# Pinning TensorE's order in the main batches of a fused attention, GLU and soft-MoE kernel

## The chip, the core and the metric

The kernel runs on one core of a Trainium2 chip. A core has five engines with a queue of instructions each: TensorE (PE in the profile; its weight loads are PEld), VectorE (DVE), ScalarE (ACT), GpSimd (POOL) and SyncE (SP), which here mostly issues transfers. TensorE writes its products to PSUM, eight banks of 128 x 512 float32, from which the other engines read them. The metric is the time of one execution in microseconds (us), lower is better; the profile describes one further execution.

## The reference

Three layers follow each other. An attention reads 8 batches of 512 tokens (8 heads of 64) against 32 states per head in both directions, which gives 512 + 32 rows of 512 numbers per batch, 4352 rows in all. A gated layer normalizes each row, multiplies it by two matrices of 512 x 1536 and combines them. A soft mixture of experts gathers 32 slots out of all rows, runs 8 experts on them and spreads the result back over the rows.

```python
a  = softmax(scale * x @ state.T);  xread = a @ state
a2 = softmax(scale * state @ x.T);  sread = a2 @ x
x  = concat([xread, sread])                          # 4352 rows of 512
xn = x / sqrt(mean(x*x) + 1e-6) * rms_g
y  = (silu(xn @ w_gate) * (xn @ w_val)) @ w_out      # 512 -> 1536 -> 512
logits = y @ phi                                     # 32 slots
d  = softmax(logits, over rows);  slot = d.T @ y     # 32 x 512
out = softmax(logits, over slots) @ experts(slot)    # 4 slots per expert
```

## The kernel before

The 4096 rows of xread are worked on in eight batches g = 0 to 7 of 512 rows; the 256 rows of sread follow as a group of their own, then the experts and the output. In a batch the gated layer runs in 12 *units* (c, t): c = 0 to 2 is a third of the 1536 columns, t = 0 to 3 a tile of 128 rows. A unit has six matmuls of 128 x 512 for the gate (`main_mm(g, c, t, 0)`, L85, tile `mm<-wp,A`), a silu on ScalarE (`main_silu`, L566, `sg`), six matmuls for the value (`main_mm(g, c, t, 1)`), and the product of both on VectorE (`main_h`, L574, `h`). The matrices `wp` are the weights multiplied by the batch's state, in a high and a low part, so they are made anew for each batch: `sw(b, c, gv)` runs two groups of small tiled products (`misc<-w,stTg`, L85), and each half is copied by ScalarE (cast, L537) and then subtracted by VectorE (L538). There are six `sw` per batch.

TensorE's other work per batch, all of it through the `misc` banks: `h_T` (L111), four transpositions of an h tile, copied to `hT` by ScalarE or VectorE (L585); `lg_mm`, the logits of a third of the columns (into a bank of its own, `lg`); `post2` and `post3`, the softmax over rows kept up to date, with small VectorE and ScalarE operations (L630 to L656) and the transpositions of E and L (L669, L670); `slot_h`, three products of h with E; and the steps of the attention for the next two batches: `att_gram`, `att_b1` (transpositions of sT), `att_b2` (`misc<-xn,e2T`), `att_b3` (transposition of srd, which VectorE computes in L360), `att_q` (`misc<-A,G`), `att_v`, `att_ss`, and `att_a3` (`misc<-xT,stT`: two banks, each read by a maximum on VectorE, L255 `cm`, and then a copy on ScalarE, L257). `c_exp` and `post_exp` run exponentials on ScalarE, for which it loads another table (ACT_TABLE_LOAD) and back again for the silu.

The program is written as `stages`: stage 0 has the 16 units of batch 0 and of the first third of batch 1, stage 1 the other 8 units of batch 1, and stages 2 to 7 one batch each. Which extra step is written beside which unit stands in `plan`, filled by `at(u, slot, step)`: slot 1 lies between a unit's gate and value products, slot 2 behind it. `next_turned()` picks up to two units whose h is turned (`h_T`) inside a later unit. The written order is only where a scheduler starts from: apart from the start of the program it orders each engine's instructions itself, by its own idea of what is ready. PSUM has four banks for the main products (`mmps`), three for all else (`misc`) and one for the logits.

Of the kernel before, what the change touches and what calls it, by code (L numbers as in the profile page):

```python
# [8 lines left out]
F32 = mybir.dt.float32  # L9
# [11 lines left out]
def kernel(  # L21
# [17 lines left out]
    B, P, H, NT, D = x_n.shape  # L39
# [38 lines left out]
    def mmps():  # L78
        return psp.tile([P, 512], F32, tag="mm", bufs=4, name="mm")

    def misc():
        return psp.tile([P, 512], F32, tag="misc", bufs=3, name="misc")
# [812 lines left out]

    for s, units in enumerate(stages):
# [67 lines left out]
        else:  # L964
            g = s
            o = 4 if s == 1 else 0
            if s == 1:
                at(0, 1, conv1)
                at(0, 2, wphi_part, 2, 1)
            nxt = [(g, 1), (g, 2)] + ([(g + 1, 0)] if g + 1 < B else [])  # L970
            for i, (nb, c) in enumerate(nxt):
                if 4 * i >= o:
                    at(4 * i - o, 2, sw, nb, c, 0)
                    at(4 * i - o + (2 if i == 1 and g > 1 else 1), 1 if i == 1 and g > 1 else 2, sw, nb, c, 1)
            if g < 7:
                at(4 if g == 1 else 1, 1, wload, 1)
                at(6 if g == 1 else 2, 2, wconv, 1)
            if g + 1 < B:
                nb = g + 1
                at(1, 1, load_xn, nb)  # L980
                at(1, 2, att_exp, nb, g > 1)
                if g > 1:
                    at(1, 2, c_exp, g - 2, True)
                    at(2, 1, c_norm, g - 2)
                at(1, 2, att_norm, nb)
                at(0, 1, att_gram, nb)
                if g > 1:
                    at(2, 2, att_b1, nb)
                    at(4, 1, att_b4, nb)
                    at(5, 2, att_b2, nb)  # L990
                    at(6, 2, att_b3, nb)
                    at(6, 2, att_q, nb, 0)
                    at(7, 1, att_q, nb, 1)
                    at(8, 2, att_v, nb)
                    at(9, 2, att_ss, nb)
                    at(10, 1, rinv, nb)
                else:
                    at(4, 2, att_b1, nb)
                    at(6, 1, att_b2, nb)
                    at(6, 2, att_b3, nb)  # L1000
                    at(5 - o // 2, 2, att_b4, nb)
                    at(6 - o // 2, 1, att_q, nb, 0)
                    at(6 - o // 2, 2, att_q, nb, 1)
                    at(7 - o // 2, 1, att_v, nb)
                    at(7 - o // 2, 2, att_ss, nb)
                    at(8 - o // 2, 1, rinv, nb)
                at(6 - o, 1, att_g, nb)
            elif g > 1:
                at(0, 1, c_exp, g - 2)
                at(0, 1, c_norm, g - 2)  # L1010
            if g + 2 < B:
                nb = g + 2
                at((8 if g > 1 else 6) - o, 1 if g > 1 else 2, load_xt, nb)
                at((10 if g > 1 else 8) - o, 1 if g > 1 else 2, att_a3, nb)
                at(11 - o, 2, att_a4, nb)
                at(10 - o, 1, att_z, nb)
            if g == B - 1:
                at(0, 2, prefetch, 2)
                at(8, 1, prefetch, 2)
                at(11, 1, w_split, 0, 0)  # L1020
                at(12, 2, w_split, 1, 0)
            if g == B - 2:
                at(8, 2, sread_prep)

        for u, (g, c, t) in enumerate(units):
# [14 lines left out]
            if ends(now):  # L1040
# [5 lines left out]
                for i in range(NC):  # L1046
                    at(u + 4, 1, slot_h, pg, i)
# [371 lines left out]
```

## Time and profile before

| | |
|---|---|
| time, median of 3 runs | 667.89 us (667.5, 667.89, 668.51) |
| the profiled execution: own time, span | 667.35 us, 665.5 us |
| mean granted TensorE clock | 0.969 |
| TensorE busy | 615.7 us, 93% of the span |
| VectorE, ScalarE, GpSimd busy | 424.4 us (64%), 338.3 us (51%), 158.3 us (24%) |
| main matmuls of the batches | 1152, 306.7 us |
| batches 2 to 7, from the first main matmul of batch 2 | 182.5 to 537.3 us |
| sread's main matmuls, then experts and output | 537.3 to 570, 570 to 665.5 us |

Busy time is the sum of an engine's instructions, without what it waits. TensorE's share is an average over stages; in the batches it is higher than at the end, where the experts' weights and the output are moved. In a timeline a row is a run of like instructions with its start and its length; the end of a run of matmuls is modelled, so the start of the next row is the surer mark. A bracket such as [0.81 <-PE misc L85] is the engine's idle time ahead of the row and what ended it.

### The profile page before, as it was taken

Reading aid. Unit: us, or ns where it says so; the run is one execution under the profiler, and the core shown is the slowest. Engines: PE = TensorE matmul, PEld = TensorE weight load, DVE = VectorE, ACT = ScalarE, POOL = GpSimd, SP = SyncE. Lnnn points to the kernel's source line nnn. Section 1 sums busy time; section 2 is a strip of 40 time slices with the busy share of each in tenths; the row PEclk is TensorE's granted clock in tenths of the full one; section 3 lists DMA queues with packets and bytes.
Section 4 is the critical chain, followed back from the end, with each engine's and each line's share of the span. In section 5 each row is a group of like instructions: output and inputs, shape, how many; then the busy total and the mean of one; then the engine's idle time right before and its main releaser. Section 6 shows DMA issues by size and latency. Waiting matters only on the chain.

```text
span 665.5 us, 11200 instructions
## 1 busy us (share of the span) xinstructions
PE 615.7 (93%) x4436; PEld 385.8 (58%) x4436; DVE 424.4 (64%) x874; ACT 338.3 (51%) x551; POOL 158.3 (24%) x178
## 2 busy tenths in 40 slices
PE   6796989999999999999999999999999999999980
PEld 4444566555656756566666666575666777653360
DVE  6969899675698566656856685686764265242170
ACT  5466784575356446434734553384445476311180
POOL 2635364532034012302210140222000000003420
PEclk9698998999999999999999999999999999999995
DMA  9950065132031212203020320300093028999757
GB/s 355 414 206 1 1 246 197 64 127 68 1 119 72 68 43 86 100 1 126 2 100 0 128 95 2 128 0 33 10 371 122 5 96 273 316 337 393 292 208 328
DMA packets 32715, 92.14 MB, mean 138 GB/s; under 512 B 1816, under 2 KB 3224, under 8 KB 29848
## 3 DMA queue, kind: packets, MB, share of 16 engines
q1 hardware_dynamic: 32376, 91.36, 37.2%
q8 instruction: 35, 0.57, 0.3%
q14 instruction: 16, 0.13, 0.1%
q10 hardware_dynamic: 288, 0.07, 0.0%
HBM read 79.37 MB, written 12.06 MB: 137 GB/s over the span
## 4 chain that ended last, share of the span: by engine, by line
PE 50%; DVE 20%; issue 18%; ACT 6%; POOL 3%; DMA 1%; DVEq 0%; POOLq 0%; ACTq 0%
PE mm L85 27%; PE misc L85 12%; PE misc L111 6%; PE so L85 2%; PE lg L85 2%; DVE h L574 2%; DVE w L212 2%; DVE wp L538 1%; POOL A L468 1%; DVE asum L326 1%; DVE wo L212 1%; DVE cm L255 1%; DVE w L208 1%; DVE w L204 1%; DVE a L268 1%
## 5 line engine op out<-in xcount | busy, mean ns | idle before, releaser
L85 PE MATMUL mm<-wp,A 128*128 128x512 f32 x1152 | 306.7, 407 | 2.3 <-ACT sg L566 1.2
L85 PEld LDWEIGHTS mm<-wp,A 128*128 128x128 f32 x1152 | 207.7, 190 | 88.1 <-issue 43.7
L566 ACT ACTIVATE sg<-mm,rinv 128x512 f32<-128x512 f32 x102 | 70.6, 692 | 105.3 <-PE mm L85 90.9
L574 DVE SCALAR_TENSOR_TENSOR h<-mm,rinv,sg 128x512 f32<-128x512 f32 x102 | 75.5, 743 | 61.6 <-PE mm L85 55.3
L538 DVE TENSOR_TENSOR wp<-misc,wp 128x512 fp32r<-128x512 f32 x96 | 62.2, 684 | 55.5 <-ACT wp L537 55.5
L537 ACT CAST wp<-misc 128x512 fp32r<-128x512 f32 x96 | 51.7, 591 | 75.6 <-PE misc L85 75.6
L85 PE MATMUL misc<-w,stTg 64*32 64x512 f32 x768 | 66.3, 611 | 10.2 <-POOL w L216 5.9
L585 ACT COPY hT<-misc 128x512 f32<-128x512 f32 x86 | 49.4, 584 | 45.2 <-PE misc L111 41.0
L111 PE MATMUL misc<-ident,h 128*128 128x128 f32 x408 | 61.0, 275 | 6.7 <-DVE h L574 6.1
L111 PEld LDWEIGHTS misc<-ident,h 128*128 128x128 f32 x408 | 48.0, 141 | 26.7 <-ACT sg L566 5.1
L511 POOL TENSOR_TENSOR rinv<-ri,rs_magic 128x4 int32<-128x4 int32 (+1 forms) x9 | 1.8, 197 | 154.9 <-DVE ri L507 154.9
L216 POOL TENSOR_TENSOR w<-w,raw 128x512 int32<-128x512 int32 x20 | 28.2, 1422 | 29.9 <-issue 8.8
L85 PEld LDWEIGHTS misc<-w,stTg 64*32 64x32 f32 x768 | 10.9, 105 | 41.6 <-issue 17.6
L85 PE MATMUL mm<-wh,xsg 128*128 128x512 f32 x96 | 31.7, 400 | 0.0
L216 POOL TENSOR_TENSOR wo<-wo,raw 128x512 int32<-128x512 int32 x18 | 24.8, 1393 | 26.7 <-DVE wo L212 20.3
L329 POOL TENSOR_TENSOR a<-a,asum 128x1024 f32<-128x1024 f32 x7 | 13.4, 1916 | 69.5 <-DVE cs L710 59.0
L85 PE MATMUL lg<-hT,wphi 128*32 128x512 f32 (+1 forms) x216 | 28.2, 578 | 0.0
L1165 POOL MEMSET sinE<- 128x512 f32 x2 | 1.0, 524 | 111.4 <-PE mm L85 101.3
L85 PE MATMUL misc<-h,ET 128*32 128x512 f32 x204 | 26.6, 597 | 0.0
L191 ACT ACTIVATE raw<-raw 128x1024 int32<-128x1024 uint32 x19 | 22.0, 1160 | 0.0
L85 PEld LDWEIGHTS mm<-wh,xsg 128*128 128x128 f32 x96 | 17.9, 188 | 6.7 <-issue 3.1
L693 DVE SCALAR_TENSOR_TENSOR acc<-acc,al,misc 128x512 f32<-128x512 f32 (+1 forms) x24 | 17.8, 746 | 4.5 <-PE misc L85 2.9
(219 smaller groups left out, 836.5 us busy)
## 6 DMA issues: line engine op xcount, KB each, us to landing
ew<-in_w_dram SPq DMA_DIRECT2D x27, 1024.0 KB, 7.3
xT<-in_x_t_dram SPq DMA_DIRECT2D x8, 1024.0 KB, 4.9
xn<-in_x_n_dram SPq DMA_DIRECT2D x8, 1024.0 KB, 4.9
raw<-in_w_val_dram SPq DMA_DIRECT2D x6, 1024.0 KB, 16.0
raw<-in_w_out_dram SPq DMA_DIRECT2D x6, 1024.0 KB, 4.9
out_dram<-ob SPq DMA_DIRECT2D x6, 1024.0 KB, 11.7
ew_w<-in_w_dram SPq DMA_DIRECT2D x5, 1024.0 KB, 10.6
raw<-in_w_gate_dram SPq DMA_DIRECT2D x4, 1024.0 KB, 13.8
```

The costliest lines, as they stand in the source:

```text
L85: nc.tensor.matmul(out=o, lhsT=lhsT, rhs=rhs, start=start, stop=stop)
L111: nc.tensor.transpose(o, i, ident)
L191: ins = nc.scalar.activation(out=rnd, in_=lo.bitcast(U32), func=AF.Copy, scale=2.0 ** -29)
L212: nc.vector.scalar_tensor_tensor(out=a[:, h], in0=hi[:, h], scalar=-0x40000000, in1=a[:, h], op0=ALU.bitwise_and, op1=ALU.bitwise_or,)
L216: nc.gpsimd.tensor_tensor(out=a[:, h], in0=a[:, h], in1=rnd[:, h], op=ALU.add)
L329: (eng or nc.gpsimd).tensor_tensor(out=a3, in0=a3, in1=asum.unsqueeze(2).to_broadcast([P, 32, 32]), op=ALU.mult)
L537: nc.scalar.copy(t[:, r, 0, :], ps)
L538: nc.vector.tensor_tensor(out=t[:, r, 1, :], in0=ps, in1=t[:, r, 0, :].bitcast(F32), op=ALU.subtract)
L566: nc.scalar.activation(out=sg, in_=ps, func=AF.Silu, scale=RINV[g][:, t : t + 1])
L574: nc.vector.scalar_tensor_tensor(out=HH[g, c][:, t, :], in0=ps, scalar=RINV[g][:, t : t + 1], in1=sg, op0=ALU.mult, op1=ALU.mult,)
L585: (nc.vector.tensor_copy if on_dve else nc.scalar.copy)(HT[g, c][:, :, t * P : (t + 1) * P], ps.rearrange("p (q n) -> p q n", q=4))
L693: nc.vector.scalar_tensor_tensor(out=acc[:np_, c, :], in0=acc[:np_, c, :], scalar=Q[g, "al"][:np_], in1=ps[:np_, :], op0=ALU.mult, op1=ALU ...
```

## The change

The change takes effect from stage 2 on, with one exception: the banks of PSUM are shared out anew for the whole program, three for main products and four for the rest. From the first unit of batch 2 to the last of batch 7 TensorE's instructions stay in the order in which they are written; the other engines are still ordered by the scheduler. Two units' main products, 24 matmuls, are written in a row; behind every second unit comes a *burst*, one of six lists per batch that `steady(g)` returns, with all of TensorE's other work. h_T and lg_mm are no longer written inside the units. The steps that don't use TensorE (loads, exponentials, norms) stay in `plan`. From batch 3 to 6, `att_b2` and `att_b3` of a batch stand in the first burst of that same batch; those of batch 7 stand in batch 6. The `else` branch of the plan, which served stages 1 to 7, keeps only what it had for stage 1 (left out below).

```diff
-        return psp.tile([P, 512], F32, tag="mm", bufs=4, name="mm")
+        return psp.tile([P, 512], F32, tag="mm", bufs=3, name="mm")
 
     def misc():
-        return psp.tile([P, 512], F32, tag="misc", bufs=3, name="misc")
+        return psp.tile([P, 512], F32, tag="misc", bufs=4, name="misc")
...
+    pe_order = ExitStack()
+
+    def steady(g):
+
+        nb, nn = g + 1, g + 2
+        last = g == B - 1
+
+        def turn(c, t, dve=False):
+            return (h_T, g, c, t, dve)
+
+        bursts = [[] for _ in range(6)]
+        b = bursts[0]
+        b += [(post2, g - 1)]
+        if not last:
+            b += [(att_gram, nb)]
+        b += [(post_exp, g - 1), (c_exp, g - 2, True)]
+        if 2 < g < B - 1:
+            b += [(att_b2, g), turn(0, 0, True), (att_b3, g)]
+        else:
+            b += [turn(0, 0, True)]
+        b += [(sw, g, 1, 0)]
+        b = bursts[1]
+        b += [(sw, g, 1, 1), (post3, g - 1), turn(0, 1), turn(0, 2)]
+        if not last:
+            b += [(att_b1, nb)]
+        b = bursts[2]
+        b += [turn(0, 3), turn(1, 0)] + [(slot_h, g - 1, i) for i in range(NC)]
+        if g == B - 2:
+            b += [(att_b2, nb)]
+        b += [(lg_mm, g, 0, 3), (sw, g, 2, 0)]
+        b = bursts[3]
+        b += [(sw, g, 2, 1)]
+        if not last:
+            b += [turn(1, 1), (att_q, nb, 0), turn(1, 2), (att_q, nb, 1)]
+        else:
+            b += [turn(1, 1), turn(1, 2)]
+        if g == B - 2:
+            b += [(att_b3, nb)]
+        b = bursts[4]
+        b += [turn(1, 3)]
+        if nn < B:
+            b += [(att_a3, nn)]
+        b += [turn(2, 0)]
+        if not last:
+            b += [(att_v, nb), (att_ss, nb), (rinv, nb), (sw, nb, 0, 0)]
+        else:
+            b += [(lg_mm, g, 1, 3)]
+        b = bursts[5]
+        if not last:
+            b += [(sw, nb, 0, 1), turn(2, 1), turn(2, 2), turn(2, 3, True)]
+            b += [(lg_mm, g, 1, 3), (lg_mm, g, 2, 3), (post1, g)]
+            if g == B - 2:
+                b += [(sread_prep,)]
+            ended.add(g)
+        else:
+            b += [turn(2, 1), turn(2, 2)]
+
+        at = lambda u, slot, f, *a: plan.setdefault((base + u, slot), []).append((f, a))
+        at(2, 1, c_norm, g - 2)
+        if not last:
+            at(1 if g == B - 2 else 7, 1, load_xn, nb)
+            at(1, 1, att_exp, nb, True)
+            at(2, 1, att_norm, nb)
+            at(4, 1, att_b4, nb)
+            at(6, 1, att_g, nb)
+            at(1, 1, wload, 1)
+            at(4, 1, wconv, 1)
+        if nn < B:
+            at(8, 1, load_xt, nn)
+            at(9, 1, att_z, nn)
+            at(11, 1, att_a4, nn)
+        if last:
+            at(0, 2, prefetch, 2)
+            at(8, 1, prefetch, 2)
+            at(11, 1, w_split, 0, 0)
+            at(12, 2, w_split, 1, 0)
+
+        return bursts
...
+                pe_order.enter_context(tc.manual_schedule(engines={mybir.EngineType.PE}))
+            bursts = steady(s)
...
-            now = next_turned()
+            now = next_turned() if s < 2 else pend[:] if (s, u) == (2, 0) else []
...
-                at(u + 1, 1, post2, pg)
-                at(u + 1, 1, post_exp, pg)
-                at(u + 2, 2, post3, pg)
-                for i in range(NC):
-                    at(u + 4, 1, slot_h, pg, i)
+                if s < 2 and u + 1 < len(units):
+                    at(u + 1, 1, post2, pg)
+                    at(u + 1, 1, post_exp, pg)
+                    at(u + 2, 2, post3, pg)
+                    for i in range(NC):
+                        at(u + 4, 1, slot_h, pg, i)
             run(2)
             pend = pend[len(now) :] + [(g, c, t)]
+            if s > 1:
+                if u % 2:
+                    for f, *a in bursts[u // 2]:
+                        f(*a)
+                pend = [(g, c, t)] if g == B - 1 and u == 11 else []
...
+        if s == B - 1:
+            pe_order.close()
```

On TensorE, in batch 4 around the third `sw` (the one that reads `w_559`), the order before has runs of six mains with a step between them:

```order
L85 MATMUL misc<-w_559,stTg 32x512 x8
L85 MATMUL mm<-wp_2809,A_2588 128x512 x6
L111 MATMUL misc<-ident,h_2991 128x128 x4
L85 MATMUL mm<-wp_2851,A_2588 128x512 x6
L111 MATMUL misc<-ident,sT 128x128 x8
L669 MATMUL misc<-ident,E 128x128
L670 MATMUL misc<-ident,L 128x128
L85 MATMUL mm<-wp_2809,A_2588 128x512 x6
L85 MATMUL mm<-wp_2851,A_2588 128x512 x6
L85 MATMUL mm<-wp_2997,A_2588 128x512 x5
```

In the changed kernel the same place, batch 4's second burst between two rows of 24 mains, reads as follows. Each `sw` and each pair of `h_T` or sT products takes two banks, one for every four matmuls:

```order
L85 MATMUL mm<-wp_2839,A_2570 128x512 x6
L85 MATMUL mm<-wp_2893,A_2570 128x512 x6
L85 MATMUL misc<-w_559,stTg 32x512 x8
L669 MATMUL misc<-ident,E 128x128
L670 MATMUL misc<-ident,L 128x128
L111 MATMUL misc<-ident,h_2952 128x128 x8
L111 MATMUL misc<-ident,sT 128x128 x8
L85 MATMUL mm<-wp_3056,A_2570 128x512 x6
L85 MATMUL mm<-wp_3115,A_2570 128x512 x6
L85 MATMUL mm<-wp_3056,A_2570 128x512 x6
L85 MATMUL mm<-wp_3115,A_2570 128x512 x6
```

The tiled products of the `sw`, two h_T and the two sT products now follow each other with no main products between them, seven banks' worth of work through four banks.

On ScalarE, in batch 7 around the casts of the `sw` for the middle third of columns, the order before is (wp_4816 and wp_4882 are the gate's and the value's weights):

```order
L537 CAST wp_4816<-misc 128x512 x2
L566 ACTIVATE sg<-mm,rinv 128x512
L655 ACT_TABLE_LOAD
L655 ACTIVATE al<-dm 128x1
L650 ACTIVATE E,es<-L,nm 128x128
L537 CAST wp_4882<-misc 128x512 x2
L566 ACT_TABLE_LOAD
L566 ACTIVATE sg<-mm,rinv 128x512 x2
```

In the changed kernel the same stretch is (wp_4864 and wp_4918 are the two weights):

```order
L655 ACT_TABLE_LOAD
L655 ACTIVATE al<-dm 128x1
L650 ACTIVATE E,es<-L,nm 128x128
L701 ACTIVATE c_all<-c_all 128x128
L566 ACT_TABLE_LOAD
L566 ACTIVATE sg<-mm,rinv 128x512 x2
L537 CAST wp_4864<-misc 128x512 x2
L537 CAST wp_4918<-misc 128x512 x2
L585 COPY hT_4862<-misc 128x4x128 x2
```

The casts of both weights now stand behind two silus and both table loads, one after the other; before, a silu and the exponentials lay between them.

## Rows read from the trace of the kernel before

**Rows 1.** Windows: start:end, length; per engine busy us (instructions); clock, DMA, GB/s.

```profile
core 0: us, PE busy (x) PEld busy (x) DVE busy (x) ACT busy (x) POOL busy (x), PEclk, DMA share, GB/s
308.30:367.70 59.40, 58.11 (x459) 37.57 (x458) 39.34 (x83) 29.85 (x52) 11.97 (x11) 1.00 0.18 64
60.00:100.00 40.00, 33.94 (x231) 24.01 (x229) 36.67 (x70) 28.18 (x40) 21.02 (x16) 0.91 0.28 105
```

**Rows 2.** TensorE's waits, 182.5 to 537.3 us: total us, times, longest.

```profile
PE misc L111 <- DVE h L574: 5.4, 9, 0.9
PE misc L111 <- ACT c_all L701: 0.4, 1, 0.4
```

**Rows 3.** Timeline of batch 4: start us, length us, engine, instructions, idle before.

```profile
316.06 0.43 PE L85 MATMUL misc<-lgs,r 128*32 128x128 f32 x8
316.42 1.65 PE L85 MATMUL mm<-wp,A 128*128 128x512 f32 x6
...
318.00 1.09 PE L85 MATMUL misc<-w,stTg 64*32 64x512 f32 x16
...
319.02 1.65 PE L85 MATMUL mm<-wp,A 128*128 128x512 f32 x6
...
320.51 0.60 PE L111 MATMUL misc<-ident,h 128*128 128x128 f32 x4
...
320.86 1.63 PE L85 MATMUL mm<-wp,A 128*128 128x512 f32 x6
...
322.33 1.04 PE L111 MATMUL misc<-ident,sT 128*128 128x128 f32 x8
...
323.34 4.13 PE L85 MATMUL mm<-wp,A 128*128 128x512 f32 x17
...
327.76 2.75 PE L85 MATMUL mm<-wp,A 128*128 128x512 f32 x11
330.03 0.73 DVE L574 SCALAR_TENSOR_TENSOR h<-mm,rinv,sg 128x512 f32<-128x512 f32 x1
...
330.91 0.63 PE L111 MATMUL misc<-ident,h 128*128 128x128 f32 x4 [0.40 <-DVE h L574]
...
344.22 0.93 PE L85 MATMUL misc<-A,G 128*128 128x512 f32 x3
...
344.98 1.55 PE L85 MATMUL mm<-wp,A 128*128 128x512 f32 x6
```

**Rows 4.** Timeline: how the sw that starts at 318.00 is emptied.

```profile
319.13 1.08 ACT L537 CAST wp<-misc 128x512 fp32r<-128x512 f32 x2 [0.81 <-PE misc L85]
319.75 1.29 DVE L538 TENSOR_TENSOR wp<-misc,wp 128x512 fp32r<-128x512 f32 x2 [0.69 <-ACT wp L537]
```

**Rows 5.** Timeline: the xT products of `att_a3` and what empties them.

```profile
360.80 1.20 PE L85 MATMUL misc<-xT,stT 64*32 64x512 f32 x16
...
361.93 3.94 PE L85 MATMUL mm<-wp,A 128*128 128x512 f32 x16
...
362.73 0.68 DVE L255 TENSOR_REDUCE cm<-misc 128x1 f32<-128x512 f32 x1
...
363.45 1.26 ACT L257 COPY sT<-misc 128x512 f32<-128x512 f32 x2 [1.81 <-DVE cm L255]
```

**Rows 6.** Timeline: `post2` on VectorE, a table load, a 128x1024 operation.

```profile
316.44 1.28 ACT L655 ACT_TABLE_LOAD   x1
316.78 0.28 DVE L630 COPY L<-misc 128x128 f32<-128x128 f32 x1
...
317.68 0.15 DVE L639 COPY mrun<-cmx 128x1 f32<-128x1 f32 x1
...
322.60 1.22 DVE L326 TENSOR_REDUCE asum<-a 128x32 f32<-128x1024 f32 x1 [0.49 <-ACT a L315]
```

**Rows 7.** TensorE's waits, 0 to 182.5 us: total us, times, longest.

```profile
PE misc L85 <- DVE e2T L339: 3.8, 2, 3.1
...
PE mm L85 <- ACT sg L566: 1.2, 1, 1.2
PE mm L85 <- DVE h L574: 1.0, 1, 1.0
```

More of the change, by code (lines that the diff above doesn't have):

```diff
@@ L963 @@
             at(13, 1, att_z, 2)
-        else:
+        elif s == 1:
             g = s
[L966 to L971, printed above, removed]
+            o = 4
+            at(0, 1, conv1)
+            at(0, 2, wphi_part, 2, 1)
+            for i, (nb, c) in enumerate([(g, 1), (g, 2), (g + 1, 0)]):
@@ L972 @@
                 if 4 * i >= o:
                     at(4 * i - o, 2, sw, nb, c, 0)
[L974 to L1023, printed above, removed]
+                    at(4 * i - o + 1, 2, sw, nb, c, 1)
@@ new lines @@
+            at(4, 1, wload, 1)
+            at(6, 2, wconv, 1)
+            nb = g + 1
+            at(1, 1, load_xn, nb)
+            at(1, 2, att_exp, nb)
+            at(1, 2, att_norm, nb)
+            at(0, 1, att_gram, nb)
+            at(4, 2, att_b1, nb)
+            at(6, 1, att_b2, nb)
+            at(6, 2, att_b3, nb)
+            at(3, 2, att_b4, nb)
+            at(4, 1, att_q, nb, 0)
+            at(4, 2, att_q, nb, 1)
+            at(5, 1, att_v, nb)
+            at(5, 2, att_ss, nb)
@@ L1025 @@
+            at(6, 1, rinv, nb)
+            at(2, 1, att_g, nb)
+            nb = g + 2
+            at(2, 2, load_xt, nb)
+            at(4, 2, att_a3, nb)
+            at(6, 1, att_z, nb)
+            at(7, 2, att_a4, nb)
+        else:
+            if s == 2:
+                pe_order.enter_context(tc.manual_schedule(engines={mybir.EngineType.PE}))
+            bursts = steady(s)
         for u, (g, c, t) in enumerate(units):
```

## The prediction

> **What bounds the kernel now.** I read the windows first [rows 1]. Batch 4 (one period of the pattern that the change rewrites) takes 59.40 us and TensorE is busy for 58.11 of them, at a granted clock of 1.00; VectorE is busy for 39.34 and ScalarE for 29.85. So in this stretch only two things can move the time: what TensorE does per batch, and what it waits for. The waits of TensorE over batches 2 to 7 come next [rows 2]: ten, 5.4 + 0.4 = 5.8 us, nine of them an h_T that starts before its h is written. The timeline gives a wait's full price: the run of 11 main matmuls at 327.76 is followed at 330.91 by a transposition that waits 0.40 for an h whose write ended at 330.03 + 0.73 [rows 3]. From start to start that is 3.15; eleven matmuls at the pitch below and an ordinary change to transposes would take about 2.6. So a wait costs some 0.16 more than its printed length, and the ten cost about 7.5.
>
> Last, what a change of kind costs. A run's pitch is (323.34's 17 mains at 4.13 less 320.86's 6 at 1.63) / 11 = 0.2275, so six back to back are 1.365. From a six's start to the next kind's start it is 1.58 between two tiled products (316.42 to 318.00), 1.49 from tiled to transposes (319.02 to 320.51), 1.47 between transposes (320.86 to 322.33) [rows 3]: surcharges of 0.215, 0.125 and 0.105.
>
> **The change, part by part.** (1) *Fewer runs.* By the two orders batch 4 has 19 runs of mains before and 6 after. By what stands around them the 19 carry 2 x 0.215 (tiled on both sides), 8 x 0.125, 3 x 0.215 (transposes ahead, tiled behind, priced as the first), and 6 x 0.105: 2.7. The six after carry 4 x 0.215 + 2 x 0.105 = 1.1. Saved: 1.6. Some comes back: an h_T ahead of mains costs 0.35 (320.51 to 320.86), ahead of another transposition 0.44 (1.04 for eight less 0.60 for four) [rows 3], and about five more stand so: 0.4. Net 1.2 a batch; over six batches, taken alike, **-7.4**.
>
> (2) *The old waits.* h_T now runs at least one row of mains, 5.5 us, after its h, so the ten waits go: **-7.5**.
>
> (3) *New waits.* Between two rows of mains the other work now stands packed, and it all goes through four misc banks that VectorE and ScalarE must empty. I walked each burst with block prices from [rows 3, 4, 5]: sw 1.02 (318.00 to 319.02), h_T 0.35 or 0.44, a pair of A,G products 0.77 (344.22 to 344.98), the xT products 1.13 (360.80 to 361.93), lgs 0.36 (316.06 to 316.42). The wait that matters is that for an sw's first bank: ScalarE's cast starts 1.13 after sw (318.00 to 319.13), VectorE's subtraction 1.75 after (319.75), two of them take 1.29, one about 0.69: the bank is free 2.44 after sw's start, and TensorE restarts 0.15 after the write that it waits for (330.76 to 330.91): 2.6.
> - Burst 1: sw 1.02, E and L 0.22 (estimate: their rows overlap), h_T 0.44, then the second h_T, which reuses sw's first bank: it comes at 1.68 and goes at 2.6, 0.92 lost. The second sT product reuses sw's second bank, whose subtraction stands behind a copy and a maximum on VectorE: some 0.13 more. 1.05.
> - Burst 3: sw, h_T 0.35, A,G 0.77 = 2.14, then an h_T on sw's first bank at 2.6: 0.45.
> - Burst 5: sw and two h_T = 1.90, the third at 2.6: 0.70.
> - Burst 4: the sw of the next batch reuses a bank of the xT products. That is freed by ScalarE's copy, which waits for VectorE's maximum: the copy starts 0.72 after the maximum and takes 0.63 [rows 5]. With the maximum at its earliest, when the products end at 1.13: 1.13 + 0.72 + 0.6 + 0.15 = 2.6, against 1.13 + 0.53 (h_T ahead of a tiled product, estimate) + 0.2 = 1.85. 0.75. In batch 4 before, that maximum came only 1.93 after the products' start.
> - Burst 0: att_b3 needs srd (one VectorE operation of 0.28 there, as the L copy [rows 6]) behind post2's small operations, which end 1.77 after lgs start (316.06 to 317.68 + 0.15) and here later by some 0.2, because the row's last h stands ahead: 2.4, against lgs, gram 0.25, xn 1.03 (estimates) and h_T 0.44 = 2.1. 0.3.
> - Burst 2 begins with h_T of old units and three slots on one bank each: none.
>
> That is 3.25 for batches 3, 4 and 5 each, 9.75. Batch 2 has no att_b3 in burst 0: 2.9. Batch 6 has no xT products, but sread_prep puts a 128x1024 VectorE operation (1.22 [rows 6]) ahead in burst 5: 3.25 - 0.75 + 1.2 = 3.7. Batch 7: ScalarE's order puts the casts of sw(7, 1, 0) behind both silus of row 1 (second fence of the change), so burst 1's sw finds its bank full, about 1.8; silus behind two table loads (1.28 each [rows 6]) 0.35; lg behind its hT 0.4: 2.6. Together **+19.0**. Bounds: each wait could be gone if its evacuation starts earlier (nothing below zero: no burst does less work than its blocks), and the VectorE and ScalarE queues, which I took nearly empty at a burst's start, could add as much as a 0.7 operation ahead of each evacuation. I take 10 to 26.
>
> The Trainium skill bears on this ("TensorEngine Tiling (Array Packing)", section "PSUM Bottleneck"): tiling speeds up the matmuls but not the copies out of PSUM, which may then be the bottleneck. By the whole batch it would cost nothing here, since neither copying engine is full; by the burst it is what the terms above are made of.
>
> (4) *Three mm banks for four.* Within a row the fourth product reuses the bank of the first, whose silu (about 0.7) has more than 2.7 us to run. Cover is gone only where ScalarE's queue holds casts or copies ahead of it; my walk leaves 0.4 in row 1. 0 in batches 2 to 7, with up to 0.4 a row if not. In the head (0 to 182 us) the scheduler still orders TensorE, with three mm and four misc banks: mm waits were 1.2 + 1.0 there, and what TensorE loses between 60 and 100, where VectorE is busy for 36.67 of 40 us [rows 1], falls into a wait of 3.1 for VectorE that comes anyway [rows 7]. I take **+0.5**, between -1 (a fourth misc bank helps the sw there) and +3.
>
> (5) The sread group, experts and output are not touched: 0. More work in a row gains no clock, since it is granted in full already [rows 1]. The Trainium skill's "Perfetto Trace Analysis" ("Matmul Optimizations") advises to put matmuls back to back so that the engine gets more power; by the granted clock of these batches that has nothing to give.
>
> **Sum.** The profiled execution took 667.35 (span 665.5 and 1.85 around it), 0.54 below the median shown. 667.35 - 7.4 - 7.5 + 19.0 + 0.5 = 671.95, and on the scale of the median **672.5**. The change pays if the new waits stay below 2.5 us a batch, and I find 3.2.
>
> **Rivals.**
> *Evacuations keep up (faster).* If casts begin when sw's first half is written, some 0.5 earlier, burst 1, 3 and 5 lose 0.4, 0 and 0.2, and with the maximum of burst 4 the waits come to about 1.6 a batch, 9.6 in all: 663. For it: casts and subtractions have a whole row's slack before. Against: in the trace the cast came 1.13 after sw's start although ScalarE had waited 0.81 for it [rows 4], so it is TensorE that releases it late. With no wait at all it would be 653. It decides from under 2.3 us a batch.
> *The gains and the waits cancel (no change):* waits of 13 to 16: 666.6 to 669.2.
> *The rows stall too (slower still).* With three mm banks a row needs ScalarE's silu in time, and at a row's start that queue holds casts and hT copies of the burst before. 0.4 to 0.5 once a batch, and the head at its upper bound: 672.5 + 2.6 + 2.5, about 677. For it: a row's last product follows the burst's waits, which push ScalarE's copies back. Against: ScalarE is busy for half of the batch only [rows 1].
>
> **Chances.** My forecast (669.3 to 676) 0.54, rows that stall too 0.14, cancelling 0.15, evacuations that keep up 0.17. A measurement of this kernel tells 0.2%, 1.3 us, from no change: faster 0.17, same 0.15, slower 0.68. The range runs from 665.0 to 677.5: it leaves out most of the faster case (0.12) and the far end of the stalling one (0.07). The forecast's own range is 669.3 to 676.
>
> **What will show it.** Batches 3 to 5 at about 60.2 us in the trace of after (59.4 before, less 1.2 for runs and 1.25 for old waits, plus 3.25), with no wait for h on L111. The largest group of TensorE's waits there should be on wp L538, 0.9 in burst 1, 0.45 in burst 3, 0.7 in burst 5, then sT L257 before the sw in burst 4. Runs of 24 mains should take 5.46 plus 0.2. Wrong I am if TensorE waits less than 2.5 us a batch, if the runs of mains show gaps (three banks), or if the head ends far from 182.5.

## The result, and the profile after

The changed kernel takes 670.56 us in the median of 20 runs (668.27 to 675.93), against 668.18 for the kernel before in runs beside them. The ratio is 1.0054, with a 95% interval of 1.0031 to 1.0076: 3.6 us slower, between 2.1 and 5.1; the means lie 3.6 apart, the medians 2.4, since 8 of the 20 times form an upper group (see "Two groups of times"). Twelve further runs gave 1.0041 (1.0017 to 1.0066). The forecast was 672.5, 4.6 slower.

The profiled execution took 668.58 (span 666.8). From the first main matmul of a batch to that of the next the two traces compare so:

| stretch | before | after | difference | forecast |
|---|---|---|---|---|
| start to batch 3 | 248.85 | 247.80 | -1.05 | +0.95 |
| batches 3, 4, 5 | 59.45, 59.39, 59.43 | 59.74, 59.75, 59.75 | +0.97 | +2.4 |
| batches 6 and 7 | 59.70 + 50.48 | 61.82 + 50.39 | +2.03 | +1.4 |
| sread group to the end | 128.2 | 127.55 | -0.65 | 0 |

(The forecast column is the prediction's own terms, with 1.2 and 1.25 taken off per batch. Part of the work of batch 7, att_b2, now stands in batch 6, so these two are added up.) So by the traces the loss is 1.3 us, where 4.6 was forecast. The first row hides a shift: the first main matmul of batch 2 comes at 186.80 in place of 182.49, and batch 2 takes 61.0 in place of 66.4. With the banks alone changed it is 186.34 and 59.9, so that is the scheduler's doing with four misc banks; the last row is 127.67 with them. The window of batch 4 after, cut at those marks, answers to [rows 1]; columns as there:

```profile
307.54:367.29 59.75, 57.49 (x462) 37.96 (x458) 40.83 (x82) 30.21 (x51) 12.01 (x11) 1.00 0.19 64
```

In batch 4 TensorE is busy for 57.49 where it was busy for 58.11, and still the batch is longer: it now stands still for 2.3 us and not for 1.3. On what, the waits of TensorE from 182.5 to 537 us tell (total us, times, longest), which answer to [rows 2]:

```profile
PE misc L111 <- DVE wp L538: 5.1, 10, 0.6
PE misc L85 <- ACT sT L257: 2.9, 4, 0.7
PE misc L111 <- DVE srd L360: 1.7, 4, 0.4
PE lg L85 <- DVE hT L585: 0.8, 1, 0.8
```

The wait for h, nine times before, is gone. In its place stand the three that the prediction named, in its order. Batch 4's bursts in TensorE's timeline (start, length), which answer to [rows 3]:

```profile
314.56 0.66 PE L111 MATMUL misc<-ident,h 128*128 128x128 f32 x4
315.65 0.33 PE L111 MATMUL misc<-ident,srd 128*128 128x128 f32 x1 [0.43 <-DVE srd L360]
...
316.92 5.74 PE L85 MATMUL mm<-wp,A 128*128 128x512 f32 x24
322.59 1.09 PE L85 MATMUL misc<-w,stTg 64*32 64x512 f32 x16
...
323.89 0.60 PE L111 MATMUL misc<-ident,h 128*128 128x128 f32 x4
325.09 0.66 PE L111 MATMUL misc<-ident,h 128*128 128x128 f32 x4 [0.60 <-DVE wp L538]
...
326.49 5.74 PE L85 MATMUL mm<-wp,A 128*128 128x512 f32 x24
...
344.73 0.95 PE L85 MATMUL misc<-A,G 128*128 128x512 f32 x3
345.79 0.66 PE L111 MATMUL misc<-ident,h 128*128 128x128 f32 x4
...
354.60 0.24 PE L85 MATMUL misc<-v,r 128*32 128x4 f32 x8
355.58 1.09 PE L85 MATMUL misc<-w,stTg 64*32 64x512 f32 x16 [0.73 <-ACT sT L257]
...
363.29 1.09 PE L111 MATMUL misc<-ident,h 128*128 128x128 f32 x8
364.76 0.66 PE L111 MATMUL misc<-ident,h 128*128 128x128 f32 x4 [0.38 <-DVE wp L538]
```

Read from start to start and less the block's own price, the losses are: burst 0, 1.09 less 0.44 = 0.65; burst 1, 1.20 less 0.44 = 0.76; burst 3, 1.06 less 0.77 = 0.29 (no bracket marks it, only the distance shows it); burst 4, 0.98 less 0.2 = 0.78; burst 5, 1.47 less 0.88 = 0.59. Together 3.07; the prediction had 0.3, 1.05, 0.45, 0.75 and 0.70, 3.25. How the bank in burst 1 comes free, on ScalarE and VectorE, answers to [rows 4]:

```profile
323.72 1.07 ACT L537 CAST wp<-misc 128x512 fp32r<-128x512 f32 x2 [1.69 <-PE misc L85]
...
324.34 0.69 DVE L538 TENSOR_TENSOR wp<-misc,wp 128x512 fp32r<-128x512 f32 x1 [0.82 <-ACT wp L537]
```

The sw starts at 322.59, the cast 1.13 later, the first subtraction 1.75 later, and the h_T on that bank 2.50 later. The chain of two evacuations is as long as before; what changed is that TensorE reaches the bank again in 1.7 us. Both engines stood idle ahead of it (the two brackets): they lack no time, they are released late. The Trainium skill ("TensorEngine Tiling (Array Packing)", section "PSUM Bottleneck") says that copies out of PSUM may become the bottleneck once tiling has sped up the matmuls. This trace agrees, with 3.1 us a batch, though neither copying engine is full.

### The profile page after: what moved, and what is told of

It is laid out like the page before. It is cut to its first block, busy times and chain, and to the rows that moved or that the text cites. A ratio compares the mean times of both kernels' runs of the same rounds, so it can differ in the third digit from the quotient of the medians.

```text
span 666.8 us, 11177 instructions
## 1 busy us (share of the span) xinstructions
PE 613.4 (92%) x4436; PEld 388.9 (58%) x4436; DVE 430.3 (65%) x873; ACT 335.8 (50%) x548; POOL 159.1 (24%) x178
## 4 chain that ended last, share of the span: by engine, by line
PE 71%; DVE 18%; ACT 6%; issue 2%; DMA 1%; POOL 0%; DVEq 0%; ACTq 0%
PE mm L85 42%; PE misc L85 15%; PE misc L111 7%; PE lg L85 3%; DVE wp L538 3%; DVE w L204 2%; DVE w L212 2%; PE so L85 2%; DVE h L574 2%; DVE w L208 2%; ACT wp L537 1%; DVE wo L212 1%; DVE cm L255 1%; DMA raw_t<-in_w_gate_dram 1%; ACT L566 1%
## 5 line engine op out<-in xcount | busy, mean ns | idle before, releaser
L85 PE MATMUL mm<-wp,A 128*128 128x512 f32 x1152 | 285.0, 399 | 3.2 <-DVE h L574 2.1
L85 PEld LDWEIGHTS mm<-wp,A 128*128 128x128 f32 x1152 | 213.2, 190 | 83.6 <-issue 32.8
L85 PE MATMUL misc<-w,stTg 64*32 64x512 f32 x768 | 66.4, 620 | 11.7 <-POOL w L216 5.7
L111 PE MATMUL misc<-ident,h 128*128 128x128 f32 x408 | 58.7, 278 | 6.4 <-DVE wp L538 5.1
L111 PEld LDWEIGHTS misc<-ident,h 128*128 128x128 f32 x408 | 45.3, 140 | 29.5 <-DVE wp L538 10.3
L468 POOL TENSOR_TENSOR A<-aT,A 128x1024 fp32r<-128x1024 f32 x7 | 16.8, 2407 | 46.4 <-ACT A L467 46.4
L204 DVE TENSOR_SCALAR w<-w 128x512 f32<-128x512 f32 x24 | 17.2, 741 | 5.1 <-ACT w L188 5.1
```

What stands on the lines that cost most here:

```text
L85: nc.tensor.matmul(out=o, lhsT=lhsT, rhs=rhs, start=start, stop=stop)
L111: nc.tensor.transpose(o, i, ident)
L204: nc.vector.tensor_scalar(out=dst[:, h], in0=dst[:, h], scalar1=EXP_LO, scalar2=EXP_HI, op0=ALU.max, op1=ALU.min,)
L468: nc.gpsimd.tensor_tensor(out=A[:, :, 1, :], in0=aT, in1=A[:, :, 0, :].bitcast(F32), op=ALU.subtract)
```

## The experiments

**The banks alone.** The kernel before, its order left to the scheduler:

```diff
-        return psp.tile([P, 512], F32, tag="mm", bufs=4, name="mm")
+        return psp.tile([P, 512], F32, tag="mm", bufs=3, name="mm")
...
-        return psp.tile([P, 512], F32, tag="misc", bufs=3, name="misc")
+        return psp.tile([P, 512], F32, tag="misc", bufs=4, name="misc")
```

> The kernel before with the banks of PSUM shared out as in the changed kernel (three main, four misc), its order still the scheduler's. Theory (the banks by themselves are worth little; the changed kernel's time comes from its pinned order): 0.998 to 1.003 of before, about 667.5. Rival (three main banks make the rows stall, and this is what costs): 1.005 or more, with waits of mm on silu or h between 182 and 537 us. Second rival (the fourth misc bank gains over 1 us ahead of batch 2): below 0.998, and the first main matmul of batch 2 over 1 us earlier.

Measured 666.64, ratio 0.9977 (0.9957 to 0.9996). So the banks by themselves are a small gain, 1.5 us, and the pinned order costs more than the whole difference. The second rival is met in its first half only: the ratio is just below 0.998, but the first main matmul of batch 2 comes 3.9 us later, not earlier; that of batch 3 comes 2.6 earlier, in an execution of 663.37, the fastest of the twelve. Its batches 3 to 5 take 59.26 to 59.29, where the kernel before has 59.4 and the changed one 59.75; the waits from 182.5 to 537 us are the old ones:

```profile
PE misc L111 <- DVE h L574: 5.1, 10, 0.9
```

**The order alone.** The changed kernel with the banks of before:

```diff
-        return psp.tile([P, 512], F32, tag="mm", bufs=3, name="mm")
+        return psp.tile([P, 512], F32, tag="mm", bufs=4, name="mm")
...
-        return psp.tile([P, 512], F32, tag="misc", bufs=4, name="misc")
+        return psp.tile([P, 512], F32, tag="misc", bufs=3, name="misc")
```

> The changed kernel with the banks of before (four main, three misc). Theory (the bursts wait for misc banks that ScalarE and VectorE empty): each burst with an sw now waits with its fourth tile in place of its fifth: some 3 us more a batch, 18 in all, about 686, the waits on wp L538 about doubled. Rival (three main banks are what costs): 668 or less.

Measured 698.34, ratio 1.0451 (1.0425 to 1.0477). The rival falls. The cause stands, but I had the size at 18 us, and it is 28: the fourth misc bank is worth 28 us to the pinned order and 1.5 to the scheduler's. Burst 1 of batch 4 on TensorE:

```profile
335.73 1.09 PE L85 MATMUL misc<-w,stTg 64*32 64x512 f32 x16
...
338.22 0.66 PE L111 MATMUL misc<-ident,h 128*128 128x128 f32 x4 [1.04 <-DVE wp L538]
339.55 0.66 PE L111 MATMUL misc<-ident,h 128*128 128x128 f32 x4 [0.68 <-ACT hT L585]
```

The first h_T now waits for the sw's first bank (2.49 after its start, as ever), and the second for the copy of the first: with three banks the reuse of a reuse is late too. The sum that I made had only the first of these. Batch 4 takes 64.02, 4.3 more than in the changed kernel, where I had 3. Batches 3 and 5 take 65.65 and 65.67, since there the granted clock falls behind the same two waits (0.79 from 272 to 280 us and from 402 to 410). In batch 4 it doesn't.

**Main banks given to misc.** The changed kernel with two main banks and five others (`bufs=3` to 2 and `bufs=4` to 5 in the same two lines).

> The changed kernel with two main and five misc banks. Theory (misc banks are what the bursts lack, main banks have slack): burst 1 loses about 0.5 in place of 0.77, burst 3 and burst 5 nothing in place of 0.29 and 0.60, burst 4 nothing in place of 0.78, burst 0 stays: 1.9 a batch less, about 658 to 661. Rival (a row then needs each silu and each h within 1.37 us, and casts and hT copies of the burst stand ahead of them): 0.5 to 1 us at the start of every row, three to six a batch more, 675 to 690, with waits of mm on silu and h.

Measured 673.21, ratio 1.0107 (1.0073 to 1.0142): neither. Both halves are in its waits from 182.5 to 537 us:

```profile
PE mm L85 <- ACT sg L566: 5.6, 6, 1.8
...
PE misc L111 <- DVE wp L538: 1.0, 6, 0.2
```

The wait on wp falls from 5.1 to 1.0 and that on sT from 2.9 to nothing, as the theory has it; in exchange the rows stall on silu, about once a batch. Batches 3 to 5 take 59.95 to 59.99, 0.2 more than with three. In this trace most of the loss lies ahead: the first main matmul of batch 3 is at 256.94, against 247.80. But the profiled execution took 679.52, and the three others 672.3 to 673.3, so how much of that is usual stays open. Of the three ways to share out eight banks that were run, three and four is the best for this order.

**sw into the middle of a row.** In the changed kernel, three of the six sw:

```diff
+                if u % 2 == 0:
+                    for f, *a in mids.get(u // 2, []):
+                        f(*a)
                 if u % 2:
...
-        b += [(sw, g, 1, 1), (post3, g - 1), turn(0, 1), turn(0, 2)]
+        mids[1] = [(sw, g, 1, 1)]
+        b += [(post3, g - 1), turn(0, 1), turn(0, 2)]
...
-        b += [(sw, g, 2, 1)]
+        mids[3] = [(sw, g, 2, 1)]
...
-            b += [(sw, nb, 0, 1), turn(2, 1), turn(2, 2), turn(2, 3, True)]
+            mids[5] = [(sw, nb, 0, 1)]
+            b += [turn(2, 1), turn(2, 2), turn(2, 3, True)]
```

(`mids` is emptied for each batch.)

> The changed kernel with the sw of bursts 1, 3 and 5 written in the middle of the row ahead of them (after its first unit), so that its banks are emptied under twelve main matmuls. Theory (those waits are the distance between an sw and the tile that reuses its bank): the waits on wp L538 go (0.77 + 0.29 + 0.60 a batch), three more runs of mains cost about 0.13 each: 1.27 a batch less, about 7 in all, so about 662 beside 669 of the changed kernel. Rival (ScalarE and VectorE are short of time around the bursts, so that the wait only moves): 667 to 670, with new waits of mm on silu or h.

Measured 664.87, ratio 0.9949 (0.9927 to 0.9972). Batches 3 to 5 take 58.48 to 58.52, so 1.26 less than the changed kernel; 1.27 was expected. No wait on wp is left. Row 1 and burst 1 of batch 4:

```profile
315.73 3.06 PE L85 MATMUL mm<-wp,A 128*128 128x512 f32 x12
318.71 1.09 PE L85 MATMUL misc<-w,stTg 64*32 64x512 f32 x16
319.73 3.04 PE L85 MATMUL mm<-wp,A 128*128 128x512 f32 x12
...
324.51 5.71 PE L85 MATMUL mm<-wp,A 128*128 128x512 f32 x24
```

The same work that took 326.49 less 316.92 = 9.57 now takes 324.51 less 315.73 = 8.78: 0.79 gained, where the wait was 0.76. Burst 3 with its row gains 0.24 of 0.29, but burst 5 only 0.14 of 0.59, because another wait is left there (see "Both moves together"). So the 0.38 that is missing from 1.64 is for the most part that wait and not the price of three more runs, and that 1.26 met 1.27 is partly luck. In batch 7 the move costs: 51.21 in place of 50.39.

**att_a3 and att_b3 behind the sw.** In the changed kernel:

```diff
-            b += [(att_b2, g), turn(0, 0, True), (att_b3, g)]
+            b += [(att_b2, g), turn(0, 0, True), (sw, g, 1, 0), (att_b3, g)]
         else:
-            b += [turn(0, 0, True)]
-        b += [(sw, g, 1, 0)]
+            b += [turn(0, 0, True), (sw, g, 1, 0)]
...
-        if nn < B:
-            b += [(att_a3, nn)]
         b += [turn(2, 0)]
         if not last:
             b += [(att_v, nb), (att_ss, nb), (rinv, nb), (sw, nb, 0, 0)]
+            if nn < B:
+                b += [(att_a3, nn)]
```

> The changed kernel with att_a3 behind the sw of burst 4 and att_b3 behind the sw of burst 0. Theory (the sw of burst 4 waits for the copy of the xT products, 0.78 in each of batches 2 to 5, and att_b3 for srd, 0.64 in batches 3 to 6, and only for their places): 5.7 less, about 663. Rival (the bank is late anyway, or the sw's casts come later by it): no wait less on sT and srd but as much more on other rows, 667 to 670.

Measured 665.11, ratio 0.9942 (0.992 to 0.9963). Batches 3 to 5 take 58.14 to 58.18: 1.59 less, 1.42 expected. In burst 4 of batch 4 no product waits:

```profile
349.80 0.24 PE L85 MATMUL misc<-v,r 128*32 128x4 f32 x8
349.98 1.20 PE L85 MATMUL misc<-w,stTg 64*32 64x512 f32 x16
```

**Both moves together.**

> The changed kernel with both sets of moves: sw of bursts 1, 3 and 5 in the middle of the row ahead, att_a3 and att_b3 behind the sw. Theory (the waits are separate, each at its own place): the gains add, 1.3 and 1.6 a batch in batches 3 to 5: a batch at 56.9 in the trace, 10 to 13 less than the changed kernel, about 656 to 659. Rival (what one gives the other takes, since both queue on the same banks): 661 to 664.

Measured 660.18, ratio 0.9892 (0.9863 to 0.9921). Batches 3 to 5 take 57.41, 2.34 less than the changed kernel, where the two apart gave 1.26 + 1.59 = 2.85. What is missing stands in burst 5. Batch 4's reads so with the sw alone moved, and so with both moves:

```profile
361.15 1.84 PE L111 MATMUL misc<-ident,h 128*128 128x128 f32 x12
361.53 0.74 DVE L574 SCALAR_TENSOR_TENSOR h<-mm,rinv,sg 128x512 f32<-128x512 f32 x1
362.92 2.01 PE L85 MATMUL lg<-hT,wphi 128*32 128x512 f32 x16
```

```profile
356.97 1.03 PE L111 MATMUL misc<-ident,h 128*128 128x128 f32 x8
357.96 0.74 DVE L574 SCALAR_TENSOR_TENSOR h<-mm,rinv,sg 128x512 f32<-128x512 f32 x1
358.76 0.66 PE L111 MATMUL misc<-ident,h 128*128 128x128 f32 x4 [0.76 <-DVE h L574]
359.35 2.01 PE L85 MATMUL lg<-hT,wphi 128*32 128x512 f32 x16
```

This is burst 5 without its sw: its third h_T turns the very unit that ended the row. In the changed kernel the sw that stood ahead hid this wait. From the first h_T to lg it is 1.77 with the sw alone moved and 2.38 with both moves, 0.61 more, where 0.51 is missing; without a wait it would be some 1.4 (two h_T at 0.44, one ahead of a tiled product at 0.53). With att_a3 behind the sw VectorE comes to that h later too, 0.99 behind the first h_T and not 0.38. So the two moves are not as separate as the theory had them.

**Batch 7's first sw.** As above, and in batch 7 also:

```diff
+        elif last:
+            mids[0] = [(sw, g, 1, 0)]
+            b += [turn(0, 0, True)]
```

> As e6, and in batch 7 also the first of the two sw of the middle third in the middle of row 0, ahead of the exponentials and table loads on ScalarE. Theory (in batch 7 its casts come late because two silus and the table loads stand ahead of them): 0.6 to 1.2 less than e6, all of it in batch 7. Rival (the scheduler puts its casts behind the exponentials anyway): the same as e6 within 0.3.

Measured 656.73, ratio 0.9841 (0.9826 to 0.9855), the fastest version with the one below. In the traces batch 7 takes 51.10 where it took 52.73, 1.6 less; batches 2 to 6 are the same to 0.1. But both traces have a stretch of batch 7 at a lower clock, each in another place. With both moves it is the second half of row 1, behind a long wait; with this edit it is the first half of row 0. The windows of the two:

```profile
491.00:497.00 6.00, 6.00 (x29) 4.36 (x22) 2.64 (x5) 1.33 (x3) 0.00 (x0) 0.72 0.02 5
476.00:482.00 6.00, 6.00 (x35) 4.04 (x34) 2.68 (x13) 0.69 (x1) 0.20 (x1) 0.72 1.03 393
```

Each costs some 1.5 us (twelve mains take 4.43 and 4.52 to the next kind, and 2.9 elsewhere), so the two cancel. What the edit does is better read at burst 1's sw, in the changed kernel, with both moves and with this edit:

```profile
502.13 1.06 PE L85 MATMUL misc<-w,stTg 64*32 64x512 f32 x8
503.80 1.06 PE L85 MATMUL misc<-w,stTg 64*32 64x512 f32 x8 [0.61 <-DVE hT L585]
504.79 0.33 PE L669 MATMUL misc<-ident,E 128*128 128x128 f32 x1
```

```profile
488.37 1.06 PE L85 MATMUL misc<-w,stTg 64*32 64x512 f32 x8
...
491.66 4.59 PE L85 MATMUL mm<-wp,A 128*128 128x512 f32 x12
```

```profile
488.74 1.65 PE L85 MATMUL misc<-w,stTg 64*32 64x512 f32 x16
490.32 3.02 PE L85 MATMUL mm<-wp,A 128*128 128x512 f32 x12
```

An sw without a wait takes 1.02. It takes 2.66 in the changed kernel, so 1.64 are lost there, near the 1.8 of the prediction; 3.29 with both moves, because in mid row it comes to the full bank sooner; and 1.58 with this edit, 1.71 less. That is more than I expected of this run. The medians lie 3.4 apart; the rest is open, within the spread of the kernel with both moves (657.5 to 664.98).

**A wait of the old kind.** In the changed kernel the h_T of unit (0, 3) moves from the start of burst 2 to that of burst 1, where its h is just being written.

```diff
-        b += [(sw, g, 1, 1), (post3, g - 1), turn(0, 1), turn(0, 2)]
+        b += [turn(0, 3), (sw, g, 1, 1), (post3, g - 1), turn(0, 1), turn(0, 2)]
...
-        b += [turn(0, 3), turn(1, 0)] + [(slot_h, g - 1, i) for i in range(NC)]
+        b += [turn(1, 0)] + [(slot_h, g - 1, i) for i in range(NC)]
```

> The changed kernel with one of its h_T, that of unit (0, 3), moved from the start of burst 2 to the start of burst 1, where its h is only just being written; one wait of the kind that the kernel before had, once in each of six batches. Theory (such a wait costs its printed length and some 0.16): 0.6 to 0.8 printed, 0.8 to 1.0 a batch, about 5 us more, 674. Rival (its time is hidden, because the second h_T of that burst then waits less for its bank): 669 or less, and the waits on wp L538 of burst 1 shorter by what the new one takes.

Measured 679.69, ratio 1.0189 (1.0171 to 1.0206): twice the expected. Batches 3 to 5 take 60.93 to 61.02, 1.22 more, so the wait is not hidden. TensorE in batch 4, and behind the last burst of batch 6:

```profile
320.67 5.78 PE L85 MATMUL mm<-wp,A 128*128 128x512 f32 x24
327.36 0.66 PE L111 MATMUL misc<-ident,h 128*128 128x128 f32 x4 [0.92 <-DVE h L574]
...
496.65 8.53 PE L85 MATMUL mm<-wp,A 128*128 128x512 f32 x24
505.10 0.43 PE L85 MATMUL misc<-lgs,r 128*32 128x128 f32 x8
```

From row to h_T it is 6.69, against 5.67 to the sw in the changed kernel: 1.02 for a printed wait of 0.92, or 1.1 if one counts that a row into transpositions is 0.09 shorter than one into a tiled product [rows 3]. The rest of the 1.22 is 0.14 for an h_T ahead of a tiled product and not of another h_T, and a little more wait on wp (burst 3 loses 0.37 in place of 0.29). Beyond that, one row takes 8.45 where 24 mains take 5.67 elsewhere. The granted clock says why, in windows with the columns of [rows 1]:

```profile
490.00:500.00 10.00, 8.62 (x48) 5.81 (x47) 7.06 (x19) 2.76 (x6) 0.20 (x1) 0.79 0.61 205
500.00:505.00 5.00, 5.00 (x17) 3.78 (x16) 0.75 (x1) 1.43 (x3) 0.00 (x0) 0.74 1.03 391
```

A share of that row ran at the lower level, 1.2 GHz. Ahead of it TensorE had waited 0.6 and 0.8 and run sixteen matmuls of one column (`ones,sq`, of sread_prep). In the changed kernel's own profile the same place, with the same two waits and the same sixteen matmuls, has a clock of 1.00. So this work does not bring the fall about every time.

**Two groups of times.** Of the changed kernel's 20 times 12 lie at 668.3 to 670.7 and 8 at 673.9 to 675.9. Three runs asked whether the place just seen makes the upper group. First the changed kernel again:

> The changed kernel unaltered, once more. Its 20 times fall into two groups, 668.3 to 670.7 and 673.9 to 675.9. Theory (in some executions the granted clock falls in the last burst of batch 6, where TensorE waits three times and then has sixteen matmuls of one column, and the row behind it takes about 3 us more, as the trace of the kernel with an early h_T shows it): the two groups again, and a profile from the upper group would show a clock under 1.00 between 480 and 500 us. Rival (the groups come from the head, whose clock differs between executions): a profile from the upper group is late already at 182 us.

Measured 670.59 (12 runs, three of them at 673.9 or more). The two groups came again, but its profile is not from the upper one (671.31), so it can't tell where that arises. It shows how executions of one program differ: batches 3 to 5 take 59.77 or 59.78 in place of 59.75, and it is 2.7 us later at the first main matmul of batch 3 (250.47) and 2.7 later at the end (669.5). The distance arises between 114 and 126 us, where a VectorE operation runs beside one of GpSimd. The first profile, and this one:

```profile
114.13 5.25 POOL L216 TENSOR_TENSOR wo<-wo,raw_t 128x512 int32<-128x512 int32 x2 [3.47 <-DVE wo L212]
114.52 0.75 DVE L204 TENSOR_SCALAR wo<-wo 128x512 f32<-128x512 f32 x2
118.90 1.08 PE L85 MATMUL misc<-r,wpp 64*128 64x32 f32 x8 [1.53 <-DVE wpp L732]
```

```profile
114.13 3.08 POOL L216 TENSOR_TENSOR wo<-wo,raw_t 128x512 int32<-128x512 int32 x2 [3.49 <-ACT wo L188]
114.52 2.98 DVE L204 TENSOR_SCALAR wo<-wo 128x512 f32<-128x512 f32 x2
120.31 1.08 PE L85 MATMUL misc<-r,wpp 64*128 64x32 f32 x8 [3.02 <-DVE wpp L732]
```

In the first profile GpSimd's first operation takes 3.57 and VectorE's two 0.42 each; in this one GpSimd's takes 1.65 and VectorE's two 1.54 and 1.52. VectorE is then late with what TensorE waits for, by 1.41, and behind the wait the clock is 0.58 from 122 to 126 us, where it was 1.00. Why one engine gives way in one execution and the other in the next stays open; of all the traces here only this one and that of the last experiment have it this way.

Second, sread_prep's two 128x1024 operations on VectorE issued in the row ahead of batch 6's last burst:

```diff
-                b += [(sread_prep,)]
+                b += [(sread_prep2,)]
...
+        if g == B - 2:
+            at(8, 2, sread_prep)
```

(`sread_prep2` is the second part of `sread_prep`, from its matmuls on, as the next fence shows.)

> The changed kernel with the two 128x1024 operations of sread_prep on VectorE issued in batch 6's fifth row and no longer in its last burst; TensorE's order is unchanged. Theory: that burst loses 0.6 + 0.8 less in waits, about 1 us in all, and the clock holds there, so the upper group of times (674 to 676) goes: all runs within 666.5 to 670.5, median about 668. Rival (the upper group comes from the head): 1 us less, but both groups stay.

Measured 674.73 (11 runs, seven of them at 673.6 or more), ratio 1.0073 (1.0045 to 1.0102): a miss in both parts. The burst's waits didn't shrink (batch 6 takes 61.88 for 61.82; the wait of lg on hT is 1.1 in place of 0.8), so it did not test what it was made for, and both groups stay. Third, only the one-column matmuls moved, to burst 2 of batch 7:

```diff
+    def sread_prep2():
+        xg, sq = xsg_t["prep"]
         ps = misc()
...
+        if last:
+            b += [(sread_prep2,)]
         b += [(lg_mm, g, 0, 3), (sw, g, 2, 0)]
```

> The changed kernel with only the sixteen one-column matmuls of sread_prep (and the small operations behind them) moved from the last burst of batch 6 to the third burst of batch 7; the waits of batch 6's last burst stay. Theory (the upper group of times, 674 to 676, comes from that burst: waits and one-column matmuls in a stretch of some 8 us, after which the row behind it runs at a lower clock in some executions): no time above 672, median 668.5 to 670. Rival (the upper group has another place, in the head or elsewhere): some 3 in 10 times again at 673.9 or more, median 670 to 671.

Measured 670.1, ratio 1.0039 (1.0023 to 1.0056). The twelve times run from 668.47 to 672.76, none in the upper group, where 11 of 32 were before. That speaks for the theory. Two traces have the low clock in that place, that with the early h_T and that with all moves (476 to 482 us, above), but neither of the changed kernel's own two, so it is likely, not shown. It is not all of it either: a fall cost 1.5 to 2.8 in the traces, and the groups lie some 5 apart. The median did not fall: the lower part of the times spread upward.

The split of sread_prep together with all moves:

> All moves (sw in mid row, att_a3 and att_b3 behind the sw, batch 7's first sw in mid row) with the same split of sread_prep. Theory: 0.5 to 1 less than the kernel with all moves and batch 7's sw (656.7), so about 656. Rival (with the sw gone from that burst, its h_T waits for the last unit's h anyway, 0.76): the same as 656.7 within 0.5.

Measured 658.1, ratio 0.9833 (0.9807 to 0.9858), by the median the rival's "the same", within the noise. The traces say more. Batches 6 and 7 take 108.0 in place of 110.2, at a clock of 1.00 from 479 to 491 us, so without the fall behind the one-column matmuls; but the first main matmul of batch 3 comes at 248.42 in place of 245.20, for the most part since VectorE gave way to GpSimd at 114 us. Whether the split keeps the clock up in other executions is not shown.

## Why the prediction was right

The direction, the mechanism and the sum of the waits held; the term of the three main banks had the wrong sign, and that the time came so near is partly luck. By the traces the changed kernel is 1.3 us slower and not 4.6: batches 3 to 5 lose 0.32 each (59.75, where I had said 60.2), and the start gains 1.05 where I had a loss of 0.95. The rest up to 3.6 comes from the upper group of times, which nothing in the prediction foresaw. The median of the twelve lower times is 669.2, 1.0 above before, the upper edge of my rival of no change.

Two of the signs of being wrong were seen. The first main matmul of batch 2 is at 186.80, not near 182.5, though batch 2 more than makes up for it. And TensorE's idle time is 2.26 us in batch 4, under 2.5; only from start to start, with the restarts and the unmarked wait of burst 3, is it 3.07.

*Fewer runs, -7.4.* Without waits a batch took 59.40 - 1.25 = 58.15 before and takes 59.75 - 3.07 = 56.7 after: 1.45 less, where I had 1.2. What I took off for h_T ahead of other transpositions (0.4) was probably too much; no run takes it apart.

*Old waits, -7.5.* They are gone, and the price that I read, the printed wait and some more, was measured as 0.92 printed and 1.0 to 1.1 lost. The sentence that every h_T runs at least a row after its h was wrong for seven of twelve. Units (0, 0), (0, 2), (1, 0), (1, 2), (2, 0) and (2, 2) are turned behind their own row, with half a row of mains between, and that was enough; (2, 3) is turned with none between. It cost nothing only because the wait for the sw's bank lay over it; both moves together brought it out.

*New waits, +19.0.* Right in batches 3 to 5: 3.07 for 3.25, with the place of each. Burst 0 was set too low (0.3 for 0.65), burst 1 and 3 a little too high. Moving what waits took away about what these figures said (1.26 for 1.27, and 1.59 for 1.42). In batch 7 the wait for a full bank is 1.64 for 1.8. The break-even of 2.5 us a batch becomes 2.7 with the better price of the runs.

*Three main banks, +0.5.* The mis-sized step. I bounded it by -1 and +3, and the banks alone give -1.5 (-2.9 to -0.3): no main matmul waits in their batches, which take 59.26 to 59.29 for 59.4, and batch 3 starts earlier (2.6 us in that trace, 1.05 in the changed kernel's). The rival "the rows stall too" is not seen with three (0.2 in all), but with two it is there at once (5.6 + 0.7).

*No effect on the clock.* In the changed kernel's batches it is 1.00 in both profiles. But the reasoning stopped at "granted in full already": waits can also take it away, as they did behind batch 6 in the kernel with the early h_T, in batches 3 and 5 with the banks of before, and in batch 7 with both moves. The Trainium skill ("Perfetto Trace Analysis", section "Matmul Optimizations"), which asks for matmuls back to back, bears here the other way round than I used it. The row at 0.74 to 0.79 agrees; the same row of the changed kernel, at 1.00 behind the same waits, does not.

Banks and order taken apart: by the medians the order costs 670.6 - 666.6 = 4 us, against 19.0 - 7.4 - 7.5 = 4.1 forecast. This agreement is closer than the parts deserve, since the low clock behind batch 6 is probably in the times of the one and not of the other.

## What to carry to other kernels

When work is packed between rows of matmuls, count the banks that it passes through and how soon it comes back to one; the time from a product's start to its bank being free (here 2.5 us for a cast and a subtraction) is the distance to keep, and it is best spent under main matmuls, unless the bank ahead is emptied late: in batch 7 the sw in mid row lost 2.27 in place of 1.64. An order pinned by hand is a list of such distances: moving six entries turned 0.5% lost into 1.6% gained. A wait that is taken away may have covered another, so add gains only after they have been tried together. And look at the granted clock of each trace before a difference between two of them is put down to an edit.

## What the runs showed of the hardware

Two executions of one program had the same batches to 0.05 us and yet ended 2.7 us apart. VectorE and GpSimd ran side by side for a few us: in one execution GpSimd's operation took 3.57 and VectorE's 0.42 each, in the other 1.65 and 1.54. TensorE then waited 3.02 in place of 1.53 and had a clock of 0.58 behind it.

A wait of TensorE can cost more than its length. Behind two waits and sixteen one-column matmuls a row took 8.45 in place of 5.67, at a clock of 0.74 to 0.79; behind a wait of 1.24 twelve mains took 4.43 in place of 2.9, at 0.72. Other executions with the same waits kept 1.00, so such a fall is in some times of a kernel and not in others.
